# Large tiles on multiples of 512 bytes, and narrower score matmuls, in a decode step's forward and backward pass

## The chip, the cores and the metric

The kernel runs on one core of a Trainium2 chip. The metric is the device time of one execution in microseconds. Runs are compared with the runs of the kernel before that were made on the same chip in turn.

Terms: HBM is the large memory in which inputs and outputs lie, SBUF the core's own memory of 128 partitions, in which the program lays out tiles, pool after pool. DMA engines move rows between the two in packets: a load writes into SBUF, a store reads from it. PE is the matmul engine (TensorE), DVE is VectorE, ACT ScalarE, POOL GpSimd. The granted clock (PEclk) is the share of PE's full clock that the profile shows as granted.

## The reference, cut to what matters

Two tokens (batch 2, one position each) pass twice through a grouped-query attention layer and an MLP. The output and the gradients of all inputs are wanted.

```python
# x: [2, 1, 1024]; k_cache, v_cache: [2, 4, 16384, 128]; wq: [1024, 4096]; wo: [4096, 1024]
# w1: [1024, 3584]; w2: [3584, 1024]; all bfloat16; 32 query heads on 4 key heads
def A(x):  # attention on the cache
    q = (x @ wq) per head
    p = softmax(q @ k.T * 128 ** -0.5)
    return (p @ v) over heads @ wo
def B(x):  # MLP
    return gelu(layernorm(x) @ w1 + b1) @ w2 + b2
x = x + A(layernorm(x)); x = x + B(layernorm(x))   # twice, with the same weights and caches
# returned: x, and the vjp of it for x, k_cache, v_cache, wq, wo, w1, b1, w2, b2
```

There is almost no arithmetic per byte. The caches are 32 MB each and are read once or more for each pass over them, the weights are read several times, and gradients of 98 MB are written.

## The kernel before: the parts that matter here

Every transfer goes through tiles of 8 KB per partition. Seven of them rotate (`ld`), ten are kept (`res`). The pools are allocated one after another in the order in which they are opened, so the sizes of the first pools set where the big tiles begin.

```python
    LDW = 4096                      # bf16 elements: 8 KB per partition
    const = ctx.enter_context(tc.tile_pool(name="const", bufs=1))
    vec = ctx.enter_context(tc.tile_pool(name="vec", bufs=1))
    pers = ctx.enter_context(tc.tile_pool(name="pers", bufs=1))
    ld = ctx.enter_context(tc.tile_pool(name="ld", bufs=NLD))      # NLD = 7
    res = ctx.enter_context(tc.tile_pool(name="res", bufs=1))
    ...
    def w_load(W, j0, rb, n_cols):          # weights: rows of n_cols * 2 bytes (2, 7 or 8 KB)
        wt = ld.tile([128, LDW], BF16, name="wt", tag="ld")
        wv = wt[:, 0:rb * n_cols].rearrange("p (j n) -> p j n", j=rb)
        nc.sync.dma_start(wv, W[j0 * 128:(j0 + rb) * 128, :].rearrange("(j p) n -> p j n", p=128))
    ...
    # caches: 8 KB rows, one per partition
            nc.sync.dma_start(t[:].rearrange("p (t d) -> p t d", d=128), src[g, :, c * TC:(c + 1) * TC, :])
    ...
    # the last stage: scores of the gradient, zero-padded to 4 columns for each of 16 vectors
    def scores(i, b, kT, dp):
        wd = wide_do[chunks[i][0]]
        for j in range(8):
            t, x = b * 8 + j // 4 * 4, 3 - j % 4
            PE.matmul(dp[:, :, t:t + 4], lhsT=kT[:, j, :], rhs=wd[:, :, x:x + 4], start=(b + j == 0), stop=False)
```

In the built program the seven load tiles begin at bytes 58816, 67008, ... of each partition and the kept ones at 116160, 124352, ...: every one 448 bytes past a multiple of 512, which is 192 past a multiple of 256.

## Time and profile before

| | before |
|---|---|
| time, median of 3 first runs | 1155.29 us (1153.3 to 1155.74) |
| bytes moved | 449.30 MB, mean 390 GB/s |
| PE, DVE, ACT busy | 83%, 55%, 49% of the span |

First the DMA and clock lines of the page, in 40 slices of 28.8 us. A digit is a share in tenths; GB/s is what all 16 DMA engines of the core moved.

```profile
PEclk9988886587997886899998899998888867799795
DMA  8999999998999999999999999888999999999996
GB/s 368 418 418 418 419 418 399 396 371 329 418 418 413 419 352 373 399 372 396 376 417 409 364 365 351 330 320 316 411 422 422 417 418 420 421 416 418 424 420 241
```

Then the queues: packets, megabytes, and the share of 16 engines' span that the packets took.

```profile
q1 hardware_dynamic: 72204, 348.17, 75.9%
q0 software_dynamic: 16752, 98.59, 20.7%
```

And a table of stretches. Columns: the stretch, its length, busy time (and instructions) of PE, PE weight loads, DVE, ACT and POOL, the granted clock, the DMA share, GB/s.

```profile
core 0: us, PE busy (x) PEld busy (x) DVE busy (x) ACT busy (x) POOL busy (x), PEclk, DMA share, GB/s
40.00:160.00 120.00, 102.55 (x1993) 84.83 (x1990) 56.44 (x121) 52.84 (x236) 0.00 (x0) 0.87 1.01 418
170.00:230.00 60.00, 33.18 (x739) 26.54 (x739) 11.51 (x43) 8.33 (x52) 1.38 (x2) 0.58 1.02 398
300.00:390.00 90.00, 76.70 (x1524) 62.45 (x1517) 42.00 (x95) 38.61 (x167) 0.00 (x0) 0.91 1.01 417
720.00:800.00 80.00, 69.96 (x1322) 54.62 (x1320) 59.22 (x126) 57.15 (x108) 5.91 (x11) 0.94 0.84 319
800.00:1100.00 300.00, 263.29 (x3422) 158.44 (x3419) 230.30 (x405) 214.55 (x412) 45.46 (x76) 0.82 1.02 418
```

A DMA share of 1.01 or 1.02 is read here as engines that are never without a packet (neighbouring packets then overlap by some 4 ns, an estimate: in 40-160 us the times of 6877 packets sum to 1.014 of 16 engines' 120 us, 3.9 ns each too much). So 40-160 and 300-390 us (cache loads alone, 8 KB rows), 170-230 us (weight loads alone, mostly 2 KB rows) and 800-1100 us (loads and gradient stores together) go at the pace of the DMA engines, and what PE does beside them should cost nothing. Around 720-800 us, at a share of 0.84, DMA has room.

The packet records of the trace say more than the rates do. They are counts of durations, not lines of the page:

```
40-160 us, loads of 8192 B:  312 ns x2901, 319 x957, 309 x441, 313 x404, ...
170-205 us, loads of 2048 B: 84 ns x950, 88 x617, 95 x401, 85 x378, ...
whole run, stores of 8192 B: 309 ns x6849 of 8192
```

Most 8 KB stores, which for the larger part run beside loads, take 309 ns. In a stretch of loads alone most packets of that size are 3 or 10 ns longer (mean 313.7), and those of 2 KB are up to 11 ns longer than 84 (mean 88.2).

The scores of the last stage (matmuls of the incoming gradient with a transposed V tile, `kT`), as a group (their mean of 211 ns is from start to end, neighbours overlapped: 896 times 211 ns is 189 us, while PE is busy with them for 55.1 us, 61.5 ns each):

```profile
L1275 PE MATMUL dp<-wdo,kT 128*128 128x64 bf16 x896 | 55.1, 211 | 0.0
```

### The profile page before, as it was taken

How to read it: one execution, taken by the hardware profiler on the slowest of the kernel's cores; microseconds unless marked ns; L12 is line 12 of the kernel's file. 1: busy time of each engine (PE TensorE's matmuls, PEld its weight loads, DVE VectorE, ACT ScalarE, POOL GpSimd, SP SyncE). 2: the span in 40 equal slices, each digit the busy share in tenths (PEclk: the TensorE clock that was granted, in tenths of full speed). 3: DMA queues.
4: the chain of work that ended last, by engine and by line, in shares of the span. 5: the costliest groups of instructions: out<-in, count | busy, mean ns of one | idle time of the engine just before them, and what ended most of it. 6: DMA issues, size and time to landing. Idle time of an engine off the chain costs nothing. (4 is left out here: it accounts for less than half of the span.)

```text
span 1151.1 us, 39972 instructions
## 1 busy us (share of the span) xinstructions
PE 952.2 (83%) x17567; PEld 735.8 (64%) x17567; DVE 633.9 (55%) x1347; ACT 566.5 (49%) x1418; POOL 64.5 (6%) x117
## 2 busy tenths in 40 slices
PE   4989886487889875899998699988898998998786
PEld 3867674487767755898876588865555554555452
DVE  1545442132544441554746454678788866787684
ACT  0544351021544440344544344767677757687573
POOL 0000000000000000000000000001111111111111
PEclk9988886587997886899998899998888867799795
DMA  8999999998999999999999999888999999999996
GB/s 368 418 418 418 419 418 399 396 371 329 418 418 413 419 352 373 399 372 396 376 417 409 364 365 351 330 320 316 411 422 422 417 418 420 421 416 418 424 420 241
DMA packets 89130, 449.30 MB, mean 390 GB/s; under 512 B 7026, under 2 KB 7026, under 8 KB 49788
## 3 DMA queue, kind: packets, MB, share of 16 engines
q1 hardware_dynamic: 72204, 348.17, 75.9%
q0 software_dynamic: 16752, 98.59, 20.7%
q8 instruction: 137, 2.24, 0.8%
q14 instruction: 37, 0.30, 0.1%
HBM read 348.14 MB, written 98.58 MB: 388 GB/s over the span
## 5 line engine op out<-in xcount | busy, mean ns | idle before, releaser
L153 ACT COPY kT<-tp 128x512 int32<-128x512 int32 x209 | 122.6, 587 | 258.9 <-PE tp L419 248.2
L156 DVE COPY kT<-tp 128x1024 bf16<-128x1024 bf16 x159 | 108.7, 690 | 111.7 <-PE tp L419 99.8
L419 PE MATMUL tp<-ident,kv_K 128*128 128x128 bf16 x1728 | 145.6, 234 | 3.3 <-DMA kv_K<-in_A_k_cache_dram 3.3
L419 PEld LDWEIGHTS <-kv_K 128*128 128x128 bf16 x1728 | 110.7, 104 | 3.9 <-DMA kv_K<-in_A_k_cache_dram 3.8
L164 DVE CAST big<-xm 128x512 bf16<-128x512 f32 x135 | 88.1, 685 | 26.4 <-PE xm L1160 13.5
L161 ACT CAST big<-xm 128x512 bf16<-128x512 f32 x162 | 88.2, 593 | 27.0 <-PE xm L1160 15.7
L572 PEld LDWEIGHTS <-kT 128*128 128x128 bf16 x2048 | 76.8, 98 | 28.0 <-issue 22.2
L572 PE MATMUL sc<-qT_bf,kT 128*128 128x8 bf16 x2048 | 92.2, 171 | 0.5 <-issue 0.4
L269 PE MATMUL wtp<-ident,wt 128*128 128x128 bf16 x928 | 77.1, 231 | 3.8 <-issue 2.5
L419 PE MATMUL tp<-ident,kv_V 128*128 128x128 bf16 x864 | 71.0, 230 | 9.8 <-DMA kv_V<-in_A_v_cache_dram 9.0
L305 PEld LDWEIGHTS <-wt 128*128 128x128 bf16 x1696 | 48.9, 103 | 47.0 <-issue 15.4
L536 ACT ACTIVATE e_all<-sc,negm 128x64 bf16<-128x64 f32 x256 | 76.9, 344 | 1.1 <-DVE negm L531 1.0
L164 DVE CAST keepK<-xm 128x512 bf16<-128x512 f32 x91 | 59.0, 685 | 22.4 <-PE xm L1242 17.7
L451 PE MATMUL acc_all<-kv_V,e_all 128*16 128x256 bf16 x864 | 46.4, 294 | 29.0 <-DMA kv_V<-in_A_v_cache_dram 16.1
L156 DVE COPY wT<-wtp 128x1024 bf16<-128x1024 bf16 (+1 forms) x64 | 40.7, 641 | 50.8 <-PE wtp L269 47.3
L161 ACT CAST keepK<-xm 128x512 bf16<-128x512 f32 x105 | 56.8, 592 | 24.2 <-PE xm L1242 21.8
L153 ACT COPY wT<-wtp 128x512 int32<-128x512 int32 (+1 forms) x60 | 34.2, 571 | 66.2 <-PE wtp L269 57.5
L419 PEld LDWEIGHTS <-kv_V 128*128 128x128 bf16 x864 | 56.1, 103 | 11.7 <-DMA kv_V<-in_A_v_cache_dram 9.8
L269 PEld LDWEIGHTS <-wt 128*128 128x128 bf16 x928 | 58.8, 103 | 4.5 <-issue 3.1
L161 ACT CAST keepV<-xm 128x512 bf16<-128x512 f32 (+1 forms) x93 | 50.3, 594 | 21.6 <-PE xm L1242 16.8
L536 ACT ACTIVATION_READ_ACCUMULATOR e_all<-sc,negm 128x1 f32 x256 | 60.2, 236 | 0.0
L164 DVE CAST keepV<-xm 128x512 bf16<-128x512 f32 (+1 forms) x80 | 52.4, 685 | 12.7 <-PE xm L1242 9.1
(350 smaller groups left out, 1774.1 us busy)
## 6 DMA issues: line engine op xcount, KB each, us to landing
kv_K<-in_A_k_cache_dram SPq DMA_DIRECT2D x81, 1024.0 KB, 12.7
kv_V<-in_A_v_cache_dram SPq DMA_DIRECT2D x81, 1024.0 KB, 12.2
out_dram<-big POOLq DMA_DIRECT2D x36, 1024.0 KB, 21.0
wt<-in_A_wo_dram SPq DMA_DIRECT2D x32, 1024.0 KB, 10.6
wt<-in_B_w_dram SPq DMA_DIRECT2D x32, 896.0 KB, 14.6
out_dram<-keepK POOLq DMA_DIRECT2D x21, 1024.0 KB, 20.0
out_dram<-keepV POOLq DMA_DIRECT2D x19, 1024.0 KB, 18.6
wt<-in_A_wq_dram SPq DMA_DIRECT2D x16, 1024.0 KB, 9.2
```

The lines of the kernel that those rows point to most:

```text
L153: S.copy(out=dst.bitcast(I32), in_=src.bitcast(I32))
L156: V.tensor_copy(out=dst, in_=src)
L161: S.copy(out=dst, in_=src)
L164: V.tensor_copy(out=dst, in_=src)
L269: PE.transpose(tp[:, o, :], wv[:, j, (o0 + o) * 128:(o0 + o + 1) * 128], ident[:])
L305: PE.matmul(fps[:, jo, :].rearrange("p (a b) -> p a b", b=2), lhsT=wv[:, j, jo * 128:(jo + 1) * 128], rhs=xT_bf[:, j0 + j, :].unsqueeze(1) ...
L419: PE.transpose(tp[:, j, :], cv[:, b * 8 + j, :], ident[:])
L451: PE.matmul(self.acc[cg:cg + 16, :], lhsT=coef(u), rhs=self.cv[:, t:t + 2, :].rearrange("p t d -> p (t d)"), start=False, stop=True, tile_ ...
L536: S.activation(out=e_all[:, g, f * half:(f + 1) * half, l, h, :], in_=sc[g][f][:, h, :].rearrange("p (a b) -> p a b", b=2), func=ACT.Exp, ...
L572: PE.matmul(sc[g][f][:, :, t % TH], lhsT=kT[:, j, :], rhs=q_bf[:, g, :], start=True, stop=True)
```

## The change

Two things. A pad of 384 bytes and a new order of the pools bring `pers`, `ld` and `res` to multiples of 512 bytes (the load tiles are then at 49664, 57856, ...). And a score matmul pads each of 16 vectors to n columns, where n is now 2 (32 columns streamed) for all chunks of the cache but the kept ones (those whose tiles stay in SBUF), which stay at 4 (64 columns). Everything else, the order of the instructions included, is the same.

```diff
-    const = ctx.enter_context(tc.tile_pool(name="const", bufs=1))
-    vec = ctx.enter_context(tc.tile_pool(name="vec", bufs=1))
+    base = ctx.enter_context(tc.tile_pool(name="base", bufs=1))
+    base.tile([128, 192], BF16, name="to512")
     pers = ctx.enter_context(tc.tile_pool(name="pers", bufs=1))
     ld = ctx.enter_context(tc.tile_pool(name="ld", bufs=NLD))
     res = ctx.enter_context(tc.tile_pool(name="res", bufs=1))
+    const = ctx.enter_context(tc.tile_pool(name="const", bufs=1))
+    vec = ctx.enter_context(tc.tile_pool(name="vec", bufs=1))
...
-    def scores(i, b, kT, dp):
+    def scores(i, b, kT, dp, n=2):
         wd = wide_do[chunks[i][0]]
         for j in range(8):
-            t, x = b * 8 + j // 4 * 4, 3 - j % 4
-            PE.matmul(dp[:, :, t:t + 4], lhsT=kT[:, j, :], rhs=wd[:, :, x:x + 4], start=(b + j == 0), stop=False)
+            t, x = b * 8 + j // n * n, 3 - j % n
+            PE.matmul(dp[:, :, t:t + n], lhsT=kT[:, j, :], rhs=wd[:, :, x:x + n], start=(b + j == 0), stop=False)
...
-            scores(c, b, kept_vT(c)[:, b * 8:(b + 1) * 8, :], dp)
+            scores(c, b, kept_vT(c)[:, b * 8:(b + 1) * 8, :], dp, 4)
```

## The prediction

> **What bounds the kernel now.** The DMA engines, in most of the span. The page's slices show it. The table of stretches shows a DMA share of 1.01 to 1.03 (saturated) at 0-240, 280-400, 440-500, 600-640 and 800-1120 us. It is lower at 240-280, 400-440, 720-800 (0.84) and after 1120 (0.63). PE is 83% busy, mostly beside a full DMA.
>
> Packet records: an 8192-byte packet takes at best 309 ns, 4096 bytes 159, 2048 bytes 84, 4 bytes 9, and neighbours on an engine overlap by about 4 ns. So each packet costs 1.18 ns per 32 bytes plus about 4 ns. [...] In stretches of loads alone packets are longer than that floor: 8 KB packets follow a pattern 312, 312, 312, 319 ns (mean about 315), 2 KB ones average 88.5 instead of 84. The extra is 4 to 5 ns per packet whatever its size. In the mixed stretch (800-1120) loads and stores both sit on the floor, 309 and 159.
>
> **What the change does.** (1) Addresses. In the program before, load and kept tiles begin 192 bytes past a multiple of 256 (448 past one of 512). After, a 384-byte pad and the new pool order put them on multiples of 512. [...] Not for reads of SBUF: stores from misaligned tiles, and 2 KB stores from a row that is aligned already, show the same 84 ns and the same law. For writes into SBUF an extra per packet, independent of size and absent where stores interleave[...]. I give that reading 60 to 65%.
>
> Summing the excess over the floor of up to 12 ns per load packet, divided by 16 engines: 2.2 us in 0-165, 2.3 in 165-240, 1.7 in 280-400, 5 in 400-720: 11 us in all, of which I take 8 to 10 to be on the critical path. After 800 us only 0.2 us is to be had.
>
> (2) Scores. 896 matmuls stream 32 columns instead of 64; 128 stay. They cost 61 ns of PE each now (55.1 us in all); 32 columns less is about 15 ns each, 13 to 15 us of PE. Nearly all of it lies after 800 us, where DMA is at its floor: worth 0 to 2 us, from 758-800 and the tail.
>
> **Prediction.** If alignment removes the excess: about 1145 us. If not: about 1154. Weighted: 1148, 8 in 10 within 1141 to 1156. Faster by over 2%: 0.04; within 2%: 0.94; slower by over 2%: 0.02.
>
> **What would show it.** Load-only stretches: 8 KB packets at 309 instead of 312/319, GB/s from 418 to about 423; 2 KB stretches from 398 to about 415. The first 240 us shorten by 4 us. After 800 us GB/s stays near 420 and the stretch hardly shortens. Score matmuls: about 15 ns less busy time each, more PE idle, no more.
>
> **What would make it wrong.** The 4 to 5 ns excess comes from something other than alignment (the HBM side[...]): then only (2) counts. Or alignment also lowers the floor, or the mixed stretch gains from more than packet time: then it is faster than 1140.

Passages that no trace of this case shows are cut from it, and from four expectations below; the cuts are marked. The sum: 11 us of excess in load packets, 8 to 10 of them on the critical path, so 1145 us if alignment removes it and 1154 if not, and at 60 to 65% for the first about 1148. "That reading" is this first case: load packets are longer because their rows begin off a multiple of 256 bytes. "Not for reads of SBUF" says where the author saw no such excess.

Three glosses. "At best" 309, 159, 84 and 9 ns are the durations that most packets of the changed kernel have (29553 of 30976 8 KB loads take 309); 60 of these loads took less, 307 for the most part. The 1.18 ns per 32 bytes plus 4 ns are an estimate from these durations and the overlap; the durations of 8 KB and 2 KB alone give (309 - 84) ns over 6144 bytes, 1.17 ns per 32 bytes. The 15 ns per score matmul are the author's estimate; in the trace of before 64 columns cost 61.5 ns of PE and the 128 columns of L419 84.3 ns (145.6 us over 1728), 11.4 ns per 32 columns.

## The result, and the profile after

The changed kernel is correct and takes 1143.61 us (median of 4, 1142.7 to 1145.0) beside 1155.4 us. The ratio is 0.9903, 95% interval 0.9886 to 0.992.

The same views of the changed kernel, first the slices:

```profile
PEclk9989785597989875899998799988878867976885
DMA  9999999998999989999999899888999999999995
GB/s 370 423 425 425 425 423 413 408 375 358 424 424 424 424 305 424 384 362 410 369 420 419 333 374 354 334 307 315 416 421 424 420 420 422 423 422 419 423 423 236
```

The queues and the stretches, with the columns as before:

```profile
q1 hardware_dynamic: 72204, 348.17, 75.5%
q0 software_dynamic: 16752, 98.59, 20.7%
```

```profile
40.00:160.00 120.00, 104.79 (x2032) 86.45 (x2030) 57.19 (x124) 53.78 (x237) 0.00 (x0) 0.86 1.01 424
170.00:230.00 60.00, 30.81 (x713) 25.34 (x711) 11.40 (x46) 5.47 (x34) 1.39 (x2) 0.56 1.02 410
300.00:390.00 90.00, 79.08 (x1543) 64.35 (x1541) 43.04 (x96) 42.75 (x193) 0.00 (x0) 0.89 1.01 424
720.00:800.00 80.00, 69.60 (x1264) 52.29 (x1262) 61.37 (x120) 56.51 (x108) 7.24 (x13) 0.91 0.84 321
800.00:1100.00 300.00, 268.20 (x3487) 160.21 (x3485) 231.37 (x407) 215.94 (x416) 45.35 (x76) 0.78 1.02 421
```

The score group:

```profile
L1277 PE MATMUL dp<-wdo,kT 128*128 128x32 bf16 x896 | 44.3, 190 | 0.0
```

Read these against the lines of before. Stretches of loads alone went from 418 to 424 GB/s with 8 KB rows and from 398 to 410 where rows of 2 KB prevail, with DMA just as full. The packet records show why: of the cache loads in 40-160 us 6143 of 6177 now take 309 ns, and of the 2 KB loads in 170-205 us 4058 of 4067 take 84 ns. The excess has not shrunk, it is gone. PE streams 11 us less in its score matmuls (55.1 to 44.3), yet PE busy in 800-1100 us did not fall, it rose from 263.29 to 268.20, and the granted clock there fell from 0.82 to 0.78. Over the whole span PE busy is 952.2 us before and 954.6 after. The experiments come back to that.

Where the time went, taken from the same VectorE instruction in each trace (microseconds from the start). The third column is the mean difference between three traces with misaligned tiles (before, e2, e3) and three with tiles on 256 or 512 (after, e1, e4), since one trace alone wanders by a microsecond or two per stage. The last column sums, over the load and store packets of the kernel before, their excess of up to 12 ns over the best duration of their size, divided by 16 engines.

| stage ends with | before | after | saved, mean of 3 and 3 | excess in packets before |
|---|---|---|---|---|
| q of layer 1 | 26.7 | 26.6 | 0.3 | 0.2 |
| attention of layer 1, forward | 210.7 | 206.9 | 3.6 | 3.4 |
| MLP of layer 1, forward | 262.4 | 256.3 | 1.1 | 1.1 |
| attention of layer 2, forward | 439.1 | 431.2 | 2.0 | 2.5 |
| MLP of layer 2, forward and backward | 487.2 | 479.5 | 0.3 | 1.0 |
| attention of layer 2, backward | 674.4 | 667.4 | 1.6 | 2.2 |
| MLP of layer 1, backward, and wo | 753.0 | 744.8 | 0.7 | 0.8 |
| last stage, all cache gradients | 1143.0 | 1134.0 | 0.7 | 0.5 |
| end | 1151.1 | 1143.2 | -0.7 | 0.1 |
| sum | | | 9.5 | 11.8 |

(The traced executions differ by 9.5 us on average, the timed runs of after, e1 and e4 by 9.5 to 12.) All of the 7.9 us between these two traces had come by 439 us. The last stage, a third of the span, gave next to nothing, although DMA is as full there as anywhere.

### The profile page after: what moved, and what is told of

Its sections match the earlier page's. It is cut to its first block, busy times and chain, and to the rows that moved or that the text cites. A ratio compares the mean times of both kernels' runs of the same rounds, so it can differ in the third digit from the quotient of the medians.

```text
span 1143.2 us, 39972 instructions
## 1 busy us (share of the span) xinstructions
PE 954.6 (84%) x17567; PEld 734.4 (64%) x17567; DVE 633.2 (55%) x1347; ACT 566.2 (50%) x1418; POOL 64.7 (6%) x117
## 5 line engine op out<-in xcount | busy, mean ns | idle before, releaser
L163 ACT CAST big<-xm 128x512 bf16<-128x512 f32 x162 | 88.3, 593 | 23.3 <-PE xm L1162 11.8
```

The source lines that it names most:

```text
L163: S.copy(out=dst, in_=src)
```

## The experiments

Theory: misaligned rows cost each packet some nanoseconds when one direction alone fills the DMA engines; that is the whole gain, and the narrower scores lie beside a full DMA. Rival A: the relief of PE gives a good part. Rival B: it is the order of the pools, not the remainder of the addresses. Rival C: 512 bytes are needed, 256 do not do. Theories D and E are two laws for the excess.

Times below are medians; "before" is the kernel before.

| run | large tiles mod 512 | score columns (others/kept) | us | before | ratio, 95% interval |
|---|---|---|---|---|---|
| after | 0 | 32/64 | 1143.61 | 1155.4 | 0.9903 (0.9886 to 0.992) |
| e1_align_only | 0 | 64/64 | 1143.65 | 1156.12 | 0.9898 (0.9878 to 0.9919) |
| e2_scores_only | 448, old pools | 32/64 | 1156.49 | 1156.12 | 1.0015 (0.9994 to 1.0036) |
| e3_off448 | 448, new pools | 32/64 | 1157.44 | 1156.12 | 1.0014 (0.999 to 1.0038) |
| e4_off256 | 256 | 32/64 | 1146.26 | 1156.12 | 0.9918 (0.9892 to 0.9945) |
| e5_off128 | 128 | 32/64 | 1154.3 | 1155.76 | 0.9981 (0.9963 to 0.9999) |
| e6_off64 | 64 | 32/64 | 1155.57 | 1155.76 | 0.9998 (0.9978 to 1.0019) |
| e7_off32 | 32 | 32/64 | 1158.15 | 1155.76 | 1.0017 (0.9997 to 1.0038) |
| e8_off224 | 224 | 32/64 | 1155.74 | 1155.76 | 1.0005 (0.998 to 1.0031) |
| e10_cols128 | 0 | 128/128 | 1151.16 | 1157.03 | 0.9955 (0.9917 to 0.9992) |
| e11_cols32 | 0 | 32/32 | 1144.89 | 1157.03 | 0.9887 (0.9862 to 0.9913) |
| e12_longrows (wrong) | 0 | 32/64 | 1143.53 | 1157.03 | 0.99 (0.9863 to 0.9936) |

### The two halves apart: e1 and e2

e1 is the changed kernel with the old width of the scores:

```diff
-    def scores(i, b, kT, dp, n=2):
+    def scores(i, b, kT, dp, n=4):
```

> The new addresses, but all scores stream 64 columns as before. My theory[...]: this holds nearly the whole gain, 1143 to 1146 us, and load packets sit at 309 and 84 ns. Rival A (the narrower scores relieve PE and give a good part of the gain): 1148 us or more. Stage view: the first 440 us shorten by 7 to 8 us as in the changed kernel.

e2 is the kernel before with the second and third hunk of the change alone (n = 2, and 4 for the kept chunks).

> The old pool order and addresses, but 32 columns for all but the kept chunks. My theory: 1153 to 1156 us, within 0.2% of before, since after 800 us DMA is full either way; the score matmuls take about 15 ns less busy time each and PE is idle more. Rival A: 1150 us or less. Load packets keep the 312/319 pattern.

e1 has the whole gain, e2 none of it. Rival A falls for this change, from 64 columns to 32: the addresses are the cause. The stretch of cache loads in e1 and in e2:

```profile
40.00:160.00 120.00, 102.85 (x2013) 84.25 (x2010) 56.61 (x124) 53.27 (x236) 0.00 (x0) 0.87 1.01 424
...
800.00:1100.00 300.00, 268.08 (x3473) 164.06 (x3471) 230.23 (x403) 213.98 (x411) 44.68 (x75) 0.81 1.02 422
```

```profile
40.00:160.00 120.00, 102.10 (x2003) 83.94 (x2000) 56.04 (x121) 53.25 (x236) 0.00 (x0) 0.87 1.01 418
...
800.00:1100.00 300.00, 266.68 (x3417) 159.50 (x3417) 229.28 (x404) 213.96 (x412) 45.45 (x76) 0.78 1.02 418
```

One expectation for e2 was wrong: PE is not idle more. Its PE busy in 800-1100 us is 266.68 against 263.29 before, with the granted clock at 0.78 against 0.82. The slower clock goes with less streaming, and it seems to take back what the narrower matmuls save (e10, with a clock of 0.89, shows the reverse); no run holds the clock fixed.

### The remainder, not the order: e3 and e4

Both are the changed kernel with another pad, so that order, instructions and scores are the same.

```diff
-    base.tile([128, 192], BF16, name="to512")
+    base.tile([128, 160], BF16, name="to512")     # e3: tiles begin at 448 mod 512
+    base.tile([128, 64], BF16, name="to512")      # e4: tiles begin at 256 mod 512
```

> The changed kernel with a pad of 320 instead of 384 bytes: its pool order and scores, but large tiles begin 448 bytes past a multiple of 512, as in the kernel before. My theory: the packets of 312 and 319 ns come back (mean excess 4 to 5 ns per load packet) and the time is that of e2, 1153 to 1156. Rival B (the new order of the pools, that is which tiles lie where, and not the remainder, made the gain): stays at 1142 to 1146 with packets at 309.

> The changed kernel with a pad of 128 bytes: large tiles begin 256 bytes past a multiple of 512. If 256 bytes is the boundary that counts: same as the changed kernel, 1142 to 1145, packets at 309 and 84. If 512 is needed (rival C): the 312/319 pattern is back and the time is 1153 to 1156.

e3 loses the gain entirely, with the 312 and 319 ns packets back in their old numbers (2986 and 1000 in 40-160 us). Rival B falls. e4 keeps it: 6145 of 6179 packets at 309 ns. The 2.6 us between its median and that of e1 are not resolved (its six runs spread from 1141.08 to 1152.49, and its trace has a span of 1142.8 us). Rival C falls: a multiple of 256 bytes is enough. Nothing in HBM moves between these runs, so the prediction's own doubt, an excess from the HBM side, falls too. The pad does shift the small pools as well; e9, which has none, answers that. e3, then e4:

```profile
40.00:160.00 120.00, 101.97 (x1996) 83.96 (x1993) 56.46 (x121) 52.97 (x236) 0.00 (x0) 0.88 1.01 418
```

```profile
40.00:160.00 120.00, 103.86 (x2010) 85.02 (x2007) 56.89 (x123) 53.37 (x236) 0.00 (x0) 0.86 1.01 424
```

### How the excess depends on the offset: e5 to e8

The same pad again, with 256, 224, 208 and 48 elements, which puts the tiles 128, 64, 32 and 224 bytes past a multiple of 512. Theory D is a guess: the excess grows with the offset from the multiple of 256. As an estimate it takes the trace's 1.17 ns for each 32 bytes of offset, and it is fitted to the 4.6 ns at 192 bytes, so that the first 64 bytes are free: about 2.3 ns at 128, nothing at 64 and 32, 5.8 at 224. Theory E: it is the same for all.

> The changed kernel with large tiles 128 bytes past a multiple of 512. In 40-160 us (8 KB loads alone) before moves 418.5 GB/s, the changed kernel 425: 4.6 ns[...] more per 8 KB packet. Theory D[...]: [...]421 to 422 GB/s there, and about 1148 us. Theory E[...]: 418.5 GB/s and about 1154 us.

> Large tiles 64 bytes past a multiple of 512. Theory D: [...]no excess left: 425 GB/s in 40-160 us, packets at 309 and 84, about 1144 us. Theory E: 418.5 GB/s, packets of 312 and 319, about 1154 us.

> Large tiles 32 bytes past a multiple of 512. Theory D: no excess, 425 GB/s, 1144 us. Theory E: 418.5 GB/s and 1154 us. A third outcome, slower than both, would say that a start off 64 bytes has a cost of its own.

> Large tiles 224 bytes past a multiple of 512. Theory D: [...]416 to 417 GB/s in 40-160 us, about 1156 us. Theory E: 418.5 GB/s and 1154 us.

Every one of them is as slow as before, to within 0.2% (the interval of e5, up to 0.9999, just misses 1). The most telling is 64 bytes, where D, fitted so, expected no loss at all. The order is e5 (128), e6 (64), e7 (32), e8 (224):

```profile
40.00:160.00 120.00, 101.85 (x1977) 83.52 (x1973) 55.62 (x121) 52.89 (x235) 0.00 (x0) 0.88 1.01 419
40.00:160.00 120.00, 100.46 (x1991) 82.97 (x1989) 55.84 (x120) 52.60 (x236) 0.00 (x0) 0.90 1.01 418
40.00:160.00 120.00, 100.29 (x1995) 82.81 (x1992) 55.85 (x120) 52.80 (x236) 0.00 (x0) 0.90 1.01 417
40.00:160.00 120.00, 102.29 (x1990) 84.53 (x1987) 55.80 (x120) 52.46 (x236) 0.00 (x0) 0.87 1.01 417
```

The mean of the 8 KB load packets in 40-160 us, those over 330 ns left out:

| bytes past 256 | 0 (after) | 0 (e4) | 32 | 64 | 128 | 192 (before) | 224 |
|---|---|---|---|---|---|---|---|
| mean ns | 309.0 | 309.0 | 314.5 | 313.6 | 312.8 | 313.7 | 314.7 |
| commonest ns | 309 | 309 | 313, 320 | 312, 319 | 309, 314 | 312, 319 | 313, 320 |

Theory D falls, E holds nearly: some 4 to 6 ns per packet whatever the offset, a nanosecond more at 32 and 224, which are not multiples of 64, and a nanosecond less at 128. Without the fit D falls as well: 1.17 ns per 32 bytes of offset would be, by estimate, 1.2, 2.3, 4.7, 7.0 and 8.2 ns in the order of the table, where 5.5, 4.6, 3.8, 4.7 and 5.7 were measured. Stores are as flat. After the last load of the kernel stores run alone, and their 4 KB packets (two rows of 2 KB) have a median of 171 or 172 ns in the traces at 32, 64, 128, 192 and 224 bytes, and of 159 in all six aligned ones. So the excess is nearly flat per row in every one of these traces. What makes it is not shown by any run.

### The disputed cost by itself: e9

A kernel without arithmetic that only moves 1 MB tiles. Its output is wrong, which doesn't matter for the time. Tiles `A` lie on multiples of 512, tiles `M` 192 bytes past one.

```python
    for k, T in enumerate((A, M)):                  # 8 KB rows, loads alone
        touch(T)                                    # VectorE separates the stretches
        for i in range(32):
            nc.sync.dma_start(T[i % 8][:], part((Kv, Vv)[k], i))
        touch(T)
    # ... then 2 KB loads, 8 KB stores, 2 KB stores, and 8 KB loads and stores together
```

> Wrong result on purpose: no arithmetic at all, only 1 MB transfers in five pairs of stretches, each pair first from or to tiles on multiples of 512, then 192 bytes past one: loads of 8 KB rows alone, loads of 2 KB rows alone, stores of 8 KB rows alone, stores of 2 KB rows alone, 8 KB loads and stores together. Theory E (about 4 to 5 ns per misaligned row when one direction runs alone): load packets 309 against a mean of 313 to 316 ns, 84 against 88 to 89; stores: the last 15 us of before, which are stores alone, show 4 KB packets at 171 to 175 instead of 159, so misaligned stores alone should cost about 6 ns per 2 KB row too, against what I predicted blind. Together: both at 309, no difference. Rival (only writes into SBUF pay, as I predicted): stores alone show no difference.

In the table of stretches the first of each pair is aligned: 8 KB loads, 2 KB loads, 8 KB stores, then both together. Columns: the stretch, its length, DVE and POOL busy, the granted clock, the DMA share, GB/s.

```profile
45.00:100.00 55.00, 0.16 (x1) 0.00 (x0) 1.00 1.01 427
130.00:180.00 50.00, 0.00 (x0) 0.00 (x0) 1.00 1.01 422
215.00:270.00 55.00, 0.31 (x2) 0.00 (x0) 1.00 1.05 409
300.00:360.00 60.00, 0.31 (x2) 0.00 (x0) 1.00 1.05 387
385.00:405.00 20.00, 0.31 (x2) 3.19 (x6) 1.00 1.01 420
435.00:455.00 20.00, 0.78 (x5) 1.59 (x3) 1.00 1.01 416
520.00:575.00 55.00, 0.00 (x0) 3.72 (x7) 1.00 1.01 428
600.00:655.00 55.00, 0.00 (x0) 3.73 (x7) 1.00 1.01 428
```

| | aligned | 192 past 256 |
|---|---|---|
| 8 KB loads alone | all 2868 packets 309 ns | mean 313.6; 312 x1212, 319 x388 |
| 2 KB loads alone | all 10976 packets 84 ns | mean 88.7; 88 x2344, 95 x1554 |
| 8 KB stores alone | median 309 | median 315 |
| 2 KB stores alone (packets of two rows) | median 159 | median 174 |
| 8 KB loads, with stores beside them | 309.0 | 309.0 |
| 8 KB stores, with loads beside them | 309.0 | 309.0 |

This settles three things. The cost is per row: 5 ns on 309 is 1% of the rate (427 to 422 GB/s), 5 ns on 84 is 5% (409 to 387). Stores alone pay as well, 15 ns for a packet of two 2 KB rows, so the rival, which was my blind reading, falls. And where loads and stores share the engines nobody pays: 428 GB/s both times. So the last stage of the kernel, loads and stores together, had next to nothing to gain (0.7 us saved there). Why the mixture is spared is not shown by any run; I leave it open.

### The width of the scores: e10 and e11

e10 streams 128 columns in every score matmul (n = 8, the padded tile 15 columns wide instead of 7, kept chunks too), e11 streams 32 in all of them:

```diff
-            scores(c, b, kept_vT(c)[:, b * 8:(b + 1) * 8, :], dp, 4)
+            scores(c, b, kept_vT(c)[:, b * 8:(b + 1) * 8, :], dp, 2)    # e11
```

> The changed kernel, but every score matmul, kept chunks too, streams 128 columns instead of 32 or 64 (more zero padding, same result). My theory, PE after 800 us stands beside a full DMA: PE busy grows by about 50 us, the time by 0 to 4 us (1143 to 1148). Rival A (the stream of the scores matters to the time): in proportion to what 32 columns should have saved, 1152 us or more.

> The changed kernel with 32 columns for the kept chunks too. Only 128 more matmuls at 741-749 us are narrower by about 12 ns each, 1.5 us of PE. Within 1142 to 1146; no difference that 3 rounds resolve.

e11 came as expected: no difference. e10 missed: 1151.16 us, outside 1143 to 1148, and its interval (up to 0.9992) does not meet that of e11 (up to 0.9913). So 128 columns cost something, though 32 and 64 cannot be told apart. In its trace, against the three aligned traces, the stage that ends at 753 us in before took 81.5 us instead of 77.3 to 79.9 (its 128 kept score matmuls run where DMA has room, at a share of 0.80 in 720-800 us), and the last stage 391.7 instead of 389.0 to 390.6. The last stage proves little, since traces with 32 columns reach 391.4 (e6) and 394.4 (e5) too. The four runs of e10 spread from 1148.43 to 1156.94, and the trace is of the fastest, so where the rest of the 7 us went is not shown. The score group and the last stretch of e10:

```profile
L1277 PE MATMUL dp<-wdo,kT 128*128 128x128 bf16 x896 | 84.1, 241 | 0.0
```

```profile
800.00:1100.00 300.00, 268.82 (x3426) 170.54 (x3423) 229.69 (x403) 213.05 (x410) 44.33 (x75) 0.89 1.02 419
```

Its scores take 39.8 us more than those of the changed kernel (84.1 to 44.3), yet PE busy in 800-1100 us is the same (268.82 and 268.20), beside a granted clock of 0.89 instead of 0.78. Over the runs the clock there follows the width: 0.77 to 0.80 with 32 columns (ten traces), 0.81 and 0.82 with 64, 0.89 with 128. So in these traces the clock goes with the columns streamed, of zero padding here, and not with PE's busy time, which is 263 to 269 us of the 300 in all of them. With one trace at 128 columns and two at 64 this is a correlation, not a test of the cause.

### Fewer packets on the aligned floor: e12

`wo` and `w2` rows are permuted so that a partition's four rows lie together and move as 8 KB instead of four times 2 KB. Its output is wrong, which doesn't matter for the time.

```diff
-        nc.sync.dma_start(wv, W[j0 * 128:(j0 + rb) * 128, :].rearrange("(j p) n -> p j n", p=128))
+        nc.sync.dma_start(wv, W[j0 * 128:(j0 + rb) * 128, :].rearrange("(p j) n -> p j n", p=128))
```

> Wrong result on purpose: the wo and w2 loads give each partition four neighbouring rows of the matrix (8 KB in one piece) in place of four rows 128 apart (2 KB each), so the rows are permuted against the vectors. It asks whether the cost per packet is what is left on the aligned floor: 23552 packets of 2 KB at 80 ns each after overlap become 5888 of 8 KB at 305, which is 5.5 us of 16 engines. About 3 to 5 us on the critical path (some of those stretches wait for PE): 1138 to 1141 us. If the packet count does not matter: 1143 to 1145.

```profile
170.00:230.00 60.00, 33.56 (x759) 27.27 (x755) 13.26 (x49) 6.56 (x42) 1.38 (x2) 0.56 1.01 421
```

The rate of 170-230 us rose from 410 to 421 GB/s, so the cost per packet is real, but the time did not move by an amount that three rounds resolve (0.99, where e11 has 0.9887). The attention stage that ends with the first of these loads took 179.4 us instead of 180.3 to 180.6, about the 1 us that 4096 packets are worth (an estimate from the expectation's figures: 80 ns each against a quarter of 305, over 16 engines); the other `wo` and `w2` loads showed nothing that could be told from the wander of a trace. My 3 to 5 us was too high, and the reason stays open. It is not that this traffic stands where DMA has room: in the trace of the changed kernel 80% of the 2 KB load packets start in stretches of 5 us in which the DMA engines are at least 95% busy (4 ns of overlap per packet taken off), and 14% in stretches under 90%. What the trace of e12 does show is longer load packets: their time beyond 309, 272 and 84 ns (for 8, 7 and 2 KB) sums to 27.2 us per engine, beside 23.0 to 25.8 in the four aligned traces after, e1, e4 and e11. So part of the 5.5 us came back as packets that were held up; why is not shown.

## Why the prediction was right or wrong

The time lies in the stated range and the verdict (within 2%) is right. That alone says little: the range of 1141 to 1156 held both outcomes, 1145 with the addresses and 1154 without, and the 1148 is a mean of the two that neither would have given. What tests the mechanism is the list of what would show it. Point by point:

- **"The DMA engines" bound most of the span, and load packets carry an excess of 4 to 5 ns that alignment may remove.** Right. After the change the excess is gone (309 and 84 ns in nearly all load packets), and e1, e2 and e3 show that the remainder of the address alone does it. The forecast of 423 GB/s for 8 KB loads came as 424, and the first stages shortened by 3.9 us (229.4 to 225.5 at the first MLP's hidden layer) where I wrote 4. In the 2 KB stretch I wrote 415 and 170-230 us shows 410.
- **The size.** I summed 11 us of excess, took 8 to 10 of it as critical, gave the reading 60 to 65%, and so put down 1148. Given the reading, my figure was "about 1145", and the measured 1143.6 is 1.4 us beyond. The gain was 11.8 us by the medians of the first comparison. The mis-sized term is the weight: the load records, with an excess per packet at two row sizes and none where stores interleave, deserved more than 60%.
- **"Not for reads of SBUF".** Wrong. e9 shows stores alone paying 15 ns per packet of two 2 KB rows. I had taken single, isolated store packets (84 ns from an aligned row) and the mixed stretch as evidence, and neither is a stretch that stores alone fill. The tail of before, with its 171 to 175 ns packets, held the answer. It cost the prediction next to nothing because so little of the kernel is stores alone: some 540 packets at the end, whose median fell from 172 to 159 ns, while the last stretch did not get shorter (8.1 us before, 8.1 to 9.3 in the aligned traces).
- **The cause behind the excess.** Not shown. Of the two laws tried, an excess that grows with the offset is not what e5 to e8 show: it is 3.8 to 5.7 ns per 8 KB row at offsets from 32 to 224 bytes, with the least, 3.8, at 128.
- **After 800 us nothing to gain.** Right: 0.7 us saved in that stage on average, and in e9 loads and stores together move 428 GB/s from tiles of either kind.
- **Scores worth 0 to 2 us.** Right in size (e2: 1.0015), but "about 15 ns less busy time each, more PE idle" is wrong in its second half. The matmuls fell by 12 ns each ((55.1 - 44.3) us over 896), and PE was no more idle, with a granted clock that fell along with the width. What fails is the step from narrower matmuls to idle PE, at a fixed clock; it cost nothing that e2 resolves (1.0015), since PE stands beside a full DMA there (share 1.02).

## What to carry to other kernels

Where a stretch is bound by DMA in one direction, look at the remainder of the SBUF addresses: rows that begin off a multiple of 256 bytes cost about 5 ns of engine time each in loads here, 1% with 8 KB rows and 5% with 2 KB rows (e9: 427 to 422 and 409 to 387 GB/s). A pad of a few hundred bytes and opening the large pools first was the whole remedy; the order alone does nothing (e3), and the pad in the old order was not run. Do not expect it to help where loads and stores run together (e9: 428 GB/s either way), and do not count on narrower matmuls to free PE before looking at the granted clock (0.82 to 0.78 here, with PE busy 263 to 268 us).
